# Float64 weights to float32: the sign by a slope of 2^32 and the low bits as integers on ScalarE

## The chip, the core and the metric

The kernel runs on one core of a Trainium2 chip. The metric is the device time of one execution in microseconds (us). A core has TensorE (PE in the profile, with its weight loads as PEld), VectorE (DVE), ScalarE (ACT), GpSimd (POOL) and SyncE (SP), which issues most of the transfers.

## What is computed

Attention with a sigmoid instead of a softmax feeds two dense layers, both of 768 to 2048 to 768 numbers for 1792 tokens:

```python
def _attn_ref(q, k, v):                     # 4 x 12 heads, 448 tokens, 64 numbers
    scores = scale * np.matmul(q, k.transpose(0, 1, 3, 2)) - np.log(S)
    return np.matmul(1.0 / (1.0 + np.exp(-scores)), v).astype(np.float32)

def _moe_ref(x, w_in, w_out):
    h = x @ w_in
    return ((h / (1.0 + np.exp(-h))) @ w_out).astype(np.float32)

def _moe2_ref(x, w_in, w_out, a, b):
    h = x @ w_in
    P = a[0] + a[1] * h + a[2] * h * h + a[3] * h * h * h
    Q = 1.0 + np.abs(b[0]) * np.abs(h) + np.abs(b[1]) * h * h
    return ((P / (Q + 1e-06)) @ w_out).astype(np.float32)
```

The four weight matrices arrive as float64, and the device reads them as pairs of 32-bit words, low word first. So the kernel itself turns 64 blocks of 128 x 768 numbers into float32: 16 blocks each of w_in and w_out of both layers.

## The kernel before

The stages follow each other on PE. Attention runs over 24 pairs of heads. The first product of layer one runs over 16 groups `g`, seven products `p1` to `p7` per group (a Strassen-like scheme, each product with nine matmuls of 448 columns, `product`, L552). The second product of layer one runs over 64 steps `n` of 18 matmuls (`second`, L699 to L701; blocks of 512, 384, 384 and 512 columns). Layer two follows with its first product (L772 to L774), the rational function, and its second product (L974). The order is written out by hand, and every engine works through its instructions in that order.

Each matmul operand is used as a high part and a rest: ACT casts a tile to the matmul type, and DVE (or POOL) subtracts that from the tile (`split`, L404 and L405; `split2`, L408 and L409; in the first product `split_later`, L414, and `flush`, L419). PE multiplies high by high, high by rest and rest by high.

A conversion of one block is issued by `conv` (L195 on). `conv_load` (L155 on) has SP load a block into a staging tile `t` of 128 x 768 x 2 words; `lo` and `hi` are its strided halves. `conv` then works in a tile `u` out of a ring of two (`bits`): ACT takes the absolute value of the high word, read as float32 (L204). DVE clamps it (L205), shifts it left by three bits and masks it (L206), puts the sign bit in (L209), and puts in the top three bits of the low word (L212). The last two read `hi` or `lo` with a stride of 8 bytes. `conv_out` (L177 on) then has SP store `u` to DRAM and load the next block; for seven blocks of w_out of layer one `conv_split` (L186 on) splits `u` at once into matmul operands instead. Both are put off to the next `conv_outs`.

With `parted=True` the last two DVE instructions are put off to `conv_rest`. The attention stage uses that form, for 12 blocks. The other 52 blocks are converted without it: 13 in the loop over `g`, one per group, and 39 in the loop over `n`, through `conv_to`, whose pace `conv_by` sets. ACT also issues the loads of `gd` and of the weights that are split in the loop over `n`.

Of the kernel before, what the change touches and what calls it, by code (L numbers as in the profile page):

```python
# [11 lines left out]
F32 = mybir.dt.float32  # L12
F32R = mybir.dt.float32r
I32 = mybir.dt.int32
AF = mybir.ActivationFunctionType
ALU = mybir.AluOpType
PSUM = bass.MemoryType.PSUM
# [5 lines left out]
MOST = (2.0 - 2.0**-3 - 2.0**-23) * 2.0**16  # L23
SIGN_TOP = -(1 << 30)
REST = 0x3FFFFFF8


class Ring:
# [13 lines left out]
def attention_moe_moe(ctx: ExitStack, tc: tile.TileContext, q, k, v, w_in1, w_out1, w_in2, w_out2, a, b2, out):  # L42
    nc = tc.nc
# [3 lines left out]
    P = 128  # L47
# [16 lines left out]
    cpool = ctx.enter_context(tc.tile_pool(name="cpool", bufs=1))  # L64
# [5 lines left out]
    def opened(name, side=None, space=None):  # L70
# [18 lines left out]
    xio = Ring([x_all[:, i, :] for i in range(3)])  # L89
    stage = Ring([t.bitcast(I32).rearrange("p (e t) -> p e t", t=2) for t in sb_[2 : 2 + NST]])  # L90
    bits = Ring(sb_[2 + NST : 4 + NST])
    xs = [[dr_p.tile([P, NT], F32, tag=f"xs{m}_{d}", name=f"xs{m}_{d}") for d in range(KD)] for m in range(2)]
    gd = [dr_p.tile([P, NT], F32, tag=f"gd{c}", name=f"gd{c}") for c in range(KF)]
    wd = [
        [{kind: dr_p.tile([P, DM], F32, tag=f"w{m}{kind}{c}", name=f"w{m}{kind}{c}") for kind in "io"} for c in range(KF)]
        for m in range(2)
    ]
# [18 lines left out]

    ident = cpool.tile([P, P], F32, tag="ident", name="ident")
    nls = cpool.tile([P, 1], F32, tag="nls", name="nls")
    ab = cpool.tile([P, 8], F32, tag="ab", name="ab")
    absb = cpool.tile([P, 2], F32, tag="absb", name="absb")  # L120
    nab = cpool.tile([P, 4], F32, tag="nab", name="nab")
# [3 lines left out]

    def constants():
        nc.vector.memset(nls, NEG_LOG_S)
        nc.vector.memset(lnb[:, 0:1], ONE * 2.0**-63)
        nc.vector.memset(lnb[:, 1:2], -63.0 * math.log(2.0))
        nc.scalar.activation(absb[:, 0:1], nls, AF.Sigmoid)  # L130
        make_identity(nc, ident)
# [6 lines left out]
    def coefficients_abs():  # L138
        nc.scalar.activation(absb, ab[:, 4:6], AF.Abs)
        nc.vector.tensor_scalar(nab, ab[:, 0:4], -1.0, 0.0, op0=ALU.mult, op1=ALU.add)  # L140

    WI = [w.bitcast(I32).rearrange("(k p) (f t) -> p k f t", p=P, t=2) for w in (w_in1, w_in2)]
    WO = [w.bitcast(I32).rearrange("(c p) (e t) -> c p e t", p=P, t=2) for w in (w_out1, w_out2)]
    order = [(0, "i", c + h * HF) for c in range(HF) for h in range(2)]
# [3 lines left out]
    staged = {}  # L150
    more = x_all.rearrange("p a b -> p (a b)").bitcast(I32).rearrange("p (e t) -> p e t", t=2)
    third = [None]
    done = {"load": 0, "conv": 0}
# [16 lines left out]
    outs = []  # L170
# [13 lines left out]
    direct = [KF]  # L184
# [8 lines left out]
    halves = []  # L193

    def conv(parted=False):  # L195
        i = done["conv"]
        if i >= len(order):
            return
        m, kind, c = order[i]
        t = staged.pop(i)  # L200
        lo, hi = t[:, :, 0], t[:, :, 1]
        u = bits.get()
        ui = u.bitcast(I32)
        nc.scalar.activation(u, hi.bitcast(F32), AF.Abs)  # L204
        nc.vector.tensor_scalar(u, u, LEAST, MOST, op0=ALU.max, op1=ALU.min)  # L205
        nc.vector.tensor_scalar(ui, ui, 3, REST, op0=ALU.logical_shift_left, op1=ALU.bitwise_and)  # L206

        def rest():
            nc.vector.scalar_tensor_tensor(  # L209
                out=ui, in0=hi, scalar=SIGN_TOP, in1=ui, op0=ALU.bitwise_and, op1=ALU.bitwise_or  # L210
            )
            nc.vector.scalar_tensor_tensor(  # L212
                out=ui, in0=lo, scalar=29, in1=ui, op0=ALU.logical_shift_right, op1=ALU.bitwise_or
            )
            outs.append(
                partial(conv_split, c, u, t)
                if (m, kind) == (0, "o") and c >= direct[0]
                else partial(conv_out, wd[m][c][kind], u, t)
            )

        done["conv"] += 1
        if parted:
            halves.append(rest)
        else:
            rest()

    def conv_rest():
        for do in halves:
# [3 lines left out]
    def conv_to(count):  # L232
        conv_outs()
        while done["conv"] < min(count, len(order)):
            conv_outs()
            conv()
# [133 lines left out]
    def attn_S(i, c, p):  # L370
        t = f2.get()
        nc.scalar.activation(t, p[:, :, :S], AF.Sigmoid, bias=nls, scale=QKSCALE)  # L372
        pairs.put(p)
# [196 lines left out]
    def silu(t, src, g, hi_f, second):  # L570
        nc.scalar.activation(t, src, AF.Silu)
        b = 2 * (g // HF) + second
        nc.sync.dma_start(out=gd[g % HF + hi_f * HF][:, b * S : (b + 1) * S], in_=t)
        f448.put(t)
# [213 lines left out]
    def act_a(n):  # L788
# [7 lines left out]
        for o, a1, _ in whole:  # L796
            nc.scalar.activation(a1, o, AF.Abs)
        nc.scalar.activation(q_, a_, AF.Identity, bias=B0, scale=B1)  # L798
# [220 lines left out]
    with tc.manual_schedule():  # L1019
# [14 lines left out]
        for i in range(4):  # L1034
            nc.vector.memset(ks_t[i][rest_of(i + 1), :, LAST * D :], 0.0)
        constants()
        warm(16)
        mix(0)
# [27 lines left out]
        for e, steps, units, new in quads():  # L1066
# [26 lines left out]
            for n in steps:  # L1093
# [30 lines left out]
                if n in CONVS:  # L1124
                    conv(True)
# [31 lines left out]
        for g in range(NGR):  # L1157
# [30 lines left out]
            if g and not HF - 1 <= g <= HF:  # L1188
                conv()
# [92 lines left out]
        for n in range(2, NL1):  # L1282
# [50 lines left out]
            m = n - (NL1 - KF)  # L1333
# [22 lines left out]
        def temps(w):  # L1356
            tm = [sb[:, i * 2 * w : (i + 1) * 2 * w] for i in range(sum(sizes) // (2 * w))]
            if w == BK:
                tm.insert(3, tm.pop(7))
            for ring, ts in ((us, tm[:4]), (aq, tm[4:8])):  # L1360
                ring.free.clear()
                ring.put(*ts)
            return tm[8:]

        rest = temps(BK)
# [6 lines left out]
        for n in range(HN):  # L1372
# [9 lines left out]
            if n == 2 * HF:  # L1382
                rest = temps(BK - P)
# [15 lines left out]
            if n == 3 * HF - 2:  # L1399
                gsrc.put(wif_all[:, NWS * HM : NWS * HM + BK])  # L1400
                load_g2(0)
                for i in range(2):
                    t = xa_all[:, 12 * BK + i * DM : 12 * BK + (i + 1) * DM]
# [88 lines left out]
```

## Time and profile before

| | us |
|---|---|
| median of 3 runs | 1035.62 |
| lowest and highest | 1034.79, 1036.03 |
| span of the profiled execution | 1036.1 |
| PE busy in it | 1026.3 |
| DVE busy in it | 783.3 |
| ACT busy in it | 606.1 |
| POOL busy in it | 273.5 |

The profile is one execution on the chip. Busy time is a sum over the span. A view by stages shows what an engine does in a stretch, the list of waits shows who stood idle until whom, and a timeline shows single instructions with their start. A matmul overlaps with the next one, so its duration in the profile is longer than the step from one start to the next; that step is its price.

### The profile page before, as it was taken

The page shows a single profiled execution, that of the slowest core. Times are in us where ns is not written, and L with a number is a line of the kernel's source. Part 1 is how long each engine was busy: PE and PEld are TensorE (multiplying, and loading weights), DVE is VectorE, ACT ScalarE, POOL GpSimd, SP SyncE. Part 2 cuts the span into 40 slices and gives each one's busy share as a digit, 9 for nine tenths or more (in the row PEclk, how much of TensorE's full clock was granted, in tenths as well). Part 3 has the DMA queues.
Part 4 walks back from the last instruction along what each step waited for, and adds up shares of the span by engine and source line. Part 5 has one row for each costly group of instructions (what it writes and reads, how often), then busy time and mean ns, then how long its engine had stood idle before and what let it go on. Part 6 is the DMA issues. An engine that isn't in the chain of part 4 may idle for free.

```text
span 1036.1 us, 16021 instructions
## 1 busy us (share of the span) xinstructions
PE 1026.3 (99%) x5568; PEld 894.5 (86%) x5568; DVE 783.3 (76%) x1101; ACT 606.1 (58%) x911; POOL 273.5 (26%) x242
## 2 busy tenths in 40 slices
PE   9999999999999999999999999999999999999998
PEld 6555547999999988899998888888999999999998
DVE  3788876888987759687867948879897968655761
ACT  5888876666655645233333458676778866454430
POOL 4335430000000000000000055778959922310000
PEclk9999999999999999999999999999999999999999
DMA  9989996777666856699989644566778878986641
GB/s 173 240 200 229 215 281 199 259 259 262 205 230 230 301 204 218 215 341 320 347 307 383 243 163 162 212 223 198 262 254 309 276 238 286 331 280 203 213 162 54
DMA packets 184081, 250.87 MB, mean 242 GB/s; under 512 B 57344, under 2 KB 136832, under 8 KB 184000
## 3 DMA queue, kind: packets, MB, share of 16 engines
q1 hardware_dynamic: 170080, 225.67, 67.5%
q10 hardware_dynamic: 11152, 17.36, 5.2%
q0 software_dynamic: 2768, 6.82, 2.9%
q8 instruction: 44, 0.72, 0.3%
q14 instruction: 37, 0.30, 0.1%
HBM read 166.17 MB, written 83.62 MB: 241 GB/s over the span
## 4 chain that ended last, share of the span: by engine, by line
PE 83%; DVE 8%; DMA 5%; ACT 2%; issue 1%; SPq 1%; POOL 0%; DVEq 0%; ACTq 0%; POOLq 0%
PE acc L552 14%; PE hp L974 14%; PE acc L701 6%; PE acc L699 6%; PE acc L700 6%; PE hb L552 5%; PE hb L974 5%; PE hp L774 5%; PE hp L772 5%; PE hp L773 5%; PE hb L381 4%; PE pair L357 3%; DMA sb<-in_moe_w_in_dram 3%; PE hb L701 2%; PE hb L700 2%; PE hb L699 2%
## 5 line engine op out<-in xcount | busy, mean ns | idle before, releaser
L204 ACT ACTIVATE sb<-sb 128x768 f32<-128x768 f32 x64 | 57.9, 905 | 72.7 <-DMA w1i<-sb 28.2
L699 PE MATMUL acc<-xa_all,woH 128*128 128x512 f32 (+1 forms) x252 | 91.9, 365 | 0.0
L700 PE MATMUL acc<-xa_all,woH 128*128 128x512 f32 (+1 forms) x252 | 91.9, 365 | 0.0
L701 PE MATMUL acc<-xa_all,woL 128*128 128x512 f32 (+1 forms) x252 | 91.9, 365 | 0.0
L372 ACT ACTIVATE sb<-pair,nls 128x896 f32<-128x896 f32 x84 | 80.1, 1006 | 7.9 <-PE pair L357 7.5
L409 POOL TENSOR_TENSOR woL<-wif,woH 128x768 fp32r<-128x768 f32 x9 | 16.5, 1848 | 248.1 <-DMA wif<-w1i 243.2
L801 POOL TENSOR_TENSOR sb<-sb 128x1024 f32<-128x1024 f32 (+1 forms) x32 | 69.6, 2174 | 39.0 <-ACT sb L798 39.0
L381 PE MATMUL hb<-sb,vs 128*64 128x448 f32 (+1 forms) x384 | 73.0, 554 | 0.0
L892 POOL TENSOR_TENSOR sb<-sb 128x384 f32<-128x384 f32 (+1 forms) x43 | 52.9, 1236 | 53.0 <-DMA sb<-gk 51.1
L552 PE MATMUL acc<-xb,wr 128*128 128x448 f32 x315 | 66.8, 362 | 0.0
L209 DVE SCALAR_TENSOR_TENSOR sb<-sb 128x768 int32<-128x768 int32 x64 | 65.3, 1021 | 1.8
L212 DVE SCALAR_TENSOR_TENSOR sb<-sb 128x768 int32<-128x768 int32 x64 | 63.3, 988 | 2.2
L552 PEld LDWEIGHTS acc<-xb,wr 128*128 128x128 f32 x315 | 59.0, 187 | 4.6 <-issue 0.7
L774 PE MATMUL hp<-hx,woL 128*128 128x512 f32 (+1 forms) x168 | 60.7, 362 | 0.0
L772 PE MATMUL hp<-hx,woH 128*128 128x512 f32 (+1 forms) x168 | 60.7, 362 | 0.0
L773 PE MATMUL hp<-hx,woH 128*128 128x512 f32 (+1 forms) x168 | 60.7, 362 | 0.0
L772 PE MATMUL hp<-xa_all,woH 128*128 128x512 f32 (+1 forms) x168 | 60.7, 362 | 0.0
L773 PE MATMUL hp<-xa_all,woH 128*128 128x512 f32 (+1 forms) x168 | 60.7, 362 | 0.0
L774 PE MATMUL hp<-xa_all,woL 128*128 128x512 f32 (+1 forms) x168 | 60.7, 362 | 0.0
L798 ACT ACTIVATE sb<-sb,absb 128x1024 f32<-128x1024 f32 (+1 forms) x32 | 36.4, 1139 | 33.5 <-DVE hb L819 33.2
L205 DVE TENSOR_SCALAR sb<-sb 128x768 f32<-128x768 f32 x64 | 36.5, 570 | 25.4 <-ACT sb L204 25.1
L803 DVE TENSOR_TENSOR sb<-hp,sb 128x768 f32<-128x768 f32 (+1 forms) x31 | 33.6, 1083 | 28.4 <-ACT sb L800 27.4
(246 smaller groups left out, 2769.9 us busy)
## 6 DMA issues: line engine op xcount, KB each, us to landing
sb<-in_moe_w_in_dram SPq DMA_DIRECT2D x32, 768.0 KB, 7.3
sb<-in_moe_w_out_dram SPq DMA_DIRECT2D x32, 768.0 KB, 6.8
gd<-sb SPq DMA_DIRECT2D x64, 224.0 KB, 3.5
wf<-w0i SPq DMA_DIRECT2D x32, 384.0 KB, 3.6
gk<-sb SPq DMA_DIRECT2D x28, 384.0 KB, 3.8
gk<-sb SPq DMA_DIRECT2D x15, 512.0 KB, 3.1
woL<-gk SPq DMA_DIRECT2D x25, 256.0 KB, 4.9
w0i<-sb SPq DMA_DIRECT2D x16, 384.0 KB, 4.0
```

Of the source, the lines that this page charges most:

```text
L209: nc.vector.scalar_tensor_tensor(out=ui, in0=hi, scalar=SIGN_TOP, in1=ui, op0=ALU.bitwise_and, op1=ALU.bitwise_or)
L372: nc.scalar.activation(t, p[:, :, :S], AF.Sigmoid, bias=nls, scale=QKSCALE)
L381: nc.tensor.matmul(hb[i_ % 2][j * D : (j + 1) * D, :S], vs[i_][part, j, c * D : (c + 1) * D], t[part, j], start=(c == 0), stop=(c == LAST),)
L552: nc.tensor.matmul(o, w_[:, w], x[:, i_, :], start=first and kk == 0 and n_ == 0, stop=kk == HK - 1 and n_ == 2, skip_group_check=not first,)
L699: nc.tensor.matmul(o, woH[c][:, w], x[:, 0, :w_], start=(c == 0), stop=False)
L700: nc.tensor.matmul(o, woH[c][:, w], x[:, 1, :w_], start=False, stop=False)
L701: nc.tensor.matmul(o, woL[c][:, w], x[:, 0, :w_], start=False, stop=(c == KF - 1))
L772: nc.tensor.matmul(o, wh[:, w], x[:, 0, :wd_], start=first, stop=False)
L773: nc.tensor.matmul(o, wh[:, w], x[:, 1, :wd_], start=False, stop=False)
L774: nc.tensor.matmul(o, wl[:, w], x[:, 0, :wd_], start=False, stop=last)
L801: nc.gpsimd.tensor_tensor(out=q_, in0=q_, in1=a_, op=ALU.mult)
L974: nc.tensor.matmul(o, a_, y[:, w_, :], start=kk_ == 0 and n_ == 0, stop=kk_ == HF - 1 and n_ == 2)
```

## The change

The conversion that is not parted gets another form. ACT's first pass scales the high word, read as float32, by 2^-112 and multiplies negative numbers by 2^32 on top (a Prelu with that slope). ACT's second pass reads the upper half of the low word as a 16-bit number x, and writes (x - 4095.5) / 8192, rounded to an integer, over the low word: its top three bits. DVE clamps the first result from both sides, and one combining instruction shifts it left by three bits and puts the three bits in. The shift drops the old sign bit; the factor 2^32 has put the sign into the exponent, from where the shift brings it to the top. A constant tile `mid` of one number per partition holds the bias of the second pass. The parted form stays as it was, and what follows a conversion (`kept_by`) is the same as before.

```diff
+DOWN = 2.0**-112
+NEGATIVE = 2.0**32
+MOST_DOWN = (2.0 - 2.0**-3 - 2.0**-23) * 2.0**-96
+EIGHTH = 2.0**-13
+MIDDLE = -4095.5 * 2.0**-13
...
+    mid = cpool.tile([P, 1], F32, tag="mid", name="mid")
...
         nc.vector.memset(nls, NEG_LOG_S)
+        nc.vector.memset(mid, MIDDLE)
...
+        kept_by = (
+            partial(conv_split, c, u, t) if (m, kind) == (0, "o") and c >= direct[0] else partial(conv_out, wd[m][c][kind], u, t)
+        )
+        done["conv"] += 1
+        if not parted:
+            nc.scalar.activation(u, hi.bitcast(F32), AF.Prelu, scale=DOWN, alpha=NEGATIVE)
+            nc.scalar.activation(lo, t.bitcast(U16)[:, :, 1], AF.Identity, bias=mid, scale=EIGHTH)
+            nc.vector.tensor_scalar(u, u, MOST_DOWN, -MOST_DOWN * NEGATIVE, op0=ALU.min, op1=ALU.max)
+            nc.vector.scalar_tensor_tensor(
+                out=ui, in0=ui, scalar=3, in1=lo, op0=ALU.logical_shift_left, op1=ALU.bitwise_or
+            )
+            outs.append(kept_by)
+            return
         nc.scalar.activation(u, hi.bitcast(F32), AF.Abs)
         nc.vector.tensor_scalar(u, u, LEAST, MOST, op0=ALU.max, op1=ALU.min)
         nc.vector.tensor_scalar(ui, ui, 3, REST, op0=ALU.logical_shift_left, op1=ALU.bitwise_and)
...
-            outs.append(
-                partial(conv_split, c, u, t)
-                if (m, kind) == (0, "o") and c >= direct[0]
-                else partial(conv_out, wd[m][c][kind], u, t)
-            )
-
-        done["conv"] += 1
-        if parted:
-            halves.append(rest)
-        else:
-            rest()
+            outs.append(kept_by)
+
+        halves.append(rest)
```

## Rows read from the trace of the kernel before

**Rows 1.** The page: busy time of the engines, and TensorE's granted clock in 40 slices.

```profile
PE 1026.3 (99%) x5568; PEld 894.5 (86%) x5568; DVE 783.3 (76%) x1101; ACT 606.1 (58%) x911; POOL 273.5 (26%) x242
...
PEclk9999999999999999999999999999999999999999
```

**Rows 2.** Busy time by stage: stretch, its length, each engine with its instructions.

```profile
163.00:373.00 210.00, 210.00 (x1048) 195.60 (x1045) 169.38 (x280) 126.59 (x229) 2.78 (x5) 1.00 0.71 238
373.00:595.00 222.00, 222.00 (x1116) 201.04 (x1115) 176.97 (x254) 90.00 (x138) 0.00 (x0) 1.00 0.84 294
```

**Rows 3.** The chain that ended last, in order of time: start, length, what.

```profile
193.89 12.60 PE acc L552 x63
```

**Rows 4.** Busy time of PE in two stretches; at the end clock, DMA share, GB/s.

```profile
377.25:426.21 48.96, 48.96 (x217) 1.00 0.67 227
433.44:477.12 43.68, 43.68 (x253) 1.00 0.98 334
```

**Rows 5.** Timeline of PE: start, length, line, tiles, form, count.

```profile
163.01 0.68 PE L552 MATMUL acc<-xb,wr 128*128 128x448 f32 x2
...
208.13 1.97 PE L552 MATMUL acc<-xa_all,wq 128*128 128x448 f32 x9
...
389.50 0.39 PE L699 MATMUL hb<-xa_all,woH 128*128 128x512 f32 x1
...
595.48 0.39 PE L772 MATMUL hb<-hx,w 128*128 128x512 f32 x1
```

**Rows 6.** Waits of PE and its weight loads, 163.1 to 595.4 us.

```profile
PEld acc L552 <- issue: 0.7, 1, 0.7
PEld hb L552 <- issue: 0.3, 1, 0.3
```

**Rows 7.** Conversions, 373 to 595 us, by line: count, busy us, mean ns, idle before.

```profile
L204 ACT ACTIVATE sb<-sb 128x768 f32<-128x768 f32 x39 | 35.4, 907 | 67.1 <-DMA w1i<-sb 28.2 <-DMA w1o<-sb 25.8 <-DVE xa_all L405 5.2
...
L212 DVE SCALAR_TENSOR_TENSOR sb<-sb 128x768 int32<-128x768 int32 x39 | 37.3, 957 | 1.4
L206 DVE TENSOR_SCALAR sb<-sb 128x768 int32<-128x768 int32 x39 | 21.9, 560 | 1.4
```

**Rows 8.** Other ACT groups by line and form.

```profile
L816 ACT ACTIVATE sb<-sb,lnb 128x768 f32<-128x768 f32 x16 | 14.8, 926 | 0.0
...
L408 ACT CAST woH<-sb 128x768 fp32r<-128x768 f32 x7 | 5.9, 836 | 15.8 <-DVE sb L212 15.8
...
L571 ACT ACT_TABLE_LOAD x1 | 1.3, 1283 | 0.0
```

**Rows 9.** Timeline of ACT in one group; in brackets the idle time before.

```profile
200.69 0.90 ACT L204 ACTIVATE sb<-sb 128x768 f32<-128x768 f32 x1
201.86 0.58 ACT L571 ACTIVATE sb<-sb 128x448 f32<-128x448 f32 x1 [0.27 <-DVE sb L426]
202.93 0.55 ACT L571 ACTIVATE sb<-acc 128x448 f32<-128x448 f32 x1 [0.49 <-PE acc L552]
203.37 0.51 ACT L414 CAST wq<-sf 128x384 fp32r<-128x384 f32 x1
204.73 0.53 ACT L627 COPY sb<-acc 128x448 f32<-128x448 f32 x1 [0.85 <-PE acc L552]
```

**Rows 10.** Timeline of DVE: the start of a conversion, and two low parts.

```profile
203.33 0.55 DVE L205 TENSOR_SCALAR sb<-sb 128x768 f32<-128x768 f32 x1
...
206.39 0.55 DVE L419 TENSOR_TENSOR wq<-sf,wq 128x384 fp32r<-128x384 f32 x1
...
388.38 0.68 DVE L405 TENSOR_TENSOR xa_all<-xa_all 128x512 fp32r<-128x512 f32 x1
```

**Rows 11.** Timeline of PE and DVE: matmuls while DVE is idle, DVE's next instruction.

```profile
368.65 0.39 PE L699 MATMUL acc<-xa_all,w 128*128 128x512 f32 x1
...
369.33 0.39 PE L699 MATMUL acc<-xa_all,w 128*128 128x512 f32 x1
...
373.38 0.62 DVE L426 TENSOR_TENSOR sb<-acc,sb 128x448 f32<-128x448 f32 x1 [7.53 <-PE acc L552]
```

More of the change, by code (lines that the diff above doesn't have):

```diff
@@ L14 @@
 I32 = mybir.dt.int32
+U16 = mybir.dt.uint16
 AF = mybir.ActivationFunctionType
```

## The prediction

> **What bounds the kernel now.** I read the page first, for the share of each engine and for TensorE's clock, and then left it, because a share over the whole span says nothing about one stage. PE is busy 99% and its granted clock is full in all 40 slices [rows 1]. Next came the table by stage [rows 2]. Of the 64 conversions, 12 run in the attention stage (0 to 163 us) in the parted form, which the change leaves alone. The other 52 lie in the two stages of the first MoE layer: 13 in its first products (163 to 373 us) and 39 in its second (373 to 595 us). Each iteration issues one or fewer of them. In both stages PE is busy the whole time, while DVE has 81% and 80% and ACT 60% and 41%.
>
> Busy PE need not be PE at its pace, so the next question is the distance from start to start. A run of 63 matmuls of 448 columns takes 12.60 us, 200.0 ns each [rows 3]. In the second stage 216 steps of 512 columns take 48.96 us, 226.7 ns each, and 252 steps of 384 columns take 43.68 us, 173.3 ns each (the counts in the rows hold one matmul more, which began before the stretch) [rows 4]. Laid end to end, 1008 x 0.2000 + 576 x 0.2267 + 576 x 0.1733 = 432.0 us. From the first matmul of the layer at 163.01 to the first of the next layer at 595.48 [rows 5] 432.5 us pass. So PE loses 0.5 us, and no more, in the whole stretch where the changed conversions run. The list of waits agrees: the only ones there are two of PE's weight loads, 0.7 and 0.3 us, put down to issue and to no engine [rows 6]. No row has PE waiting for a conversion.
>
> **The change, part by part.** All durations are from the profiled execution (span 1036.14 us; the runs have a median of 1035.62, so the trace is 0.05% above it and I take differences straight across).
>
> *Removed on DVE, for 52 conversions:* the shift with its mask (0.56 us) and one of the two combining instructions (0.96 us) [rows 7]. That is 1.52 us each, 79 us of DVE's 346 in the two stages. The clamp stays one instruction of the same form on the same tile (0.55 [rows 10]), the other combining instruction stays with the same operand layout (0.96).
>
> *Added on ACT, 52 times:* the first pass replaces the absolute value at 0.91 us; same data, same size, only the function differs. The second pass is new. No row shows a pass that reads every fourth 2-byte number and writes integers. The nearest is one of the same 768 numbers with a bias per partition, 0.93 us [rows 8], and I take that. From below, the plain cast of 768 numbers is 0.84 [rows 8]; I see no reason why it should cost nothing. From above, I allow twice the present strided pass, 1.81. So ACT gets 52 x 0.93 = 48 us (44 to 94) on top of 217.
>
> *On the path:* none of the 79 us saved is in front of PE, which loses 0.5 us in all. That is the ceiling of the gain. The cost is nil only as long as something hides it, so I checked the tightest places.
>
> First stage, one iteration. ACT does the absolute value at 200.69 and then the cast for the product p7 at 203.37; the copy of the sum at 204.73 waited 0.85 us for PE [rows 9]. DVE makes the low part of that cast at 206.39, right behind the conversion, and is done at 206.94 [rows 10]; p7 starts at 208.13 and reads the low part in its third matmul, 0.4 us later [rows 5]. The second ACT pass goes behind the first at about 201.5. Queued behind it on ACT are the two silu passes, the cast, the copy, the next weights' casts and the issues of loads; they move by at most 0.93, less the 0.27, 0.49 and 0.85 us that ACT stood waiting there [rows 9]. DVE's wait is new: its combining instruction now also needs the second ACT pass. But DVE reaches the conversion at 203.33 [rows 10], when that pass has been done for 0.9 us, and then is 1.5 us quicker. The low part moves from 206.94 to about 205.4 and the margin before p7 grows from 1.6 to about 3 us.
>
> Second stage. From the start of the ACT pass to the result a conversion took 0.91 + 0.55 + 0.56 + 0.96 + 0.96 and some gaps, 4.1 us. It becomes 0.91 + 0.93 on ACT and 0.96 behind it on DVE, 2.8 us. So SP, which issues the store of the result and then the next load, gets both 1.3 us sooner; it passes no other work, since the order on the queue is the same. ACT waits in this stage 54 us for those very stores to free a buffer [rows 7] and 16 us for DVE to finish a conversion before it casts the result [rows 8]; both waits shrink, by about as much as the pass costs. The tightest operand behind a conversion is the low part that DVE ended at 389.06 [rows 10] for a matmul at 389.50 [rows 5], 0.44 us. It came late because DVE was full; DVE is the engine that is relieved.
>
> *The rest:* the set of one constant in the first microsecond (DVE is idle until a load lands), and the small step by which the tiles allocated behind that constant move. Neither has a row; I take both as nothing.
>
> *Sum:* gain at most 0.5 us. If the new pass came whole in front of that 0.44 us twice, the loss is 2 x (0.93 - 0.44) = 1.0 us. I forecast no change, 1035.6 us.
>
> **The rivals.**
>
> *ACT becomes the bound of the second stage, slower.* The mechanism is the price of the added work per conversion there. ACT is busy 90.0 of 222 us [rows 2], so 39 conversions have room for (222 - 90) / 39 = 3.4 us each. Above that PE must wait. Against it: the row nearest to the pass is 0.93, and in the first stage even 4.7 us would still fit before p7. If the strided read and integer write were four times the present pass, 3.6 us, ACT would need 90 + 39 x 3.6 = 230 us and the time would be about 1044. The other way to that price is a reload of the function table around each new function: two loads of 1.283 us [rows 8] with the 0.93 make 3.5 us, 90 + 39 x 3.5 = 226 us, and about 1040. In its favour, the slope function appears nowhere in this trace; against it, absolute value, silu, sigmoid, casts and copies follow each other with three table loads in the whole run, of which the rows show one. The Trainium skill (ScalarE: Activation LUTs, section "Table sets: the hidden batching unit") says that tables are loaded as sets, that cheap functions such as relu, copy, identity and abs are in every set, and that a function outside the active set costs a load; it does not name the slope function among them. The trace agrees on the price, 1283 ns. Chance 0.05.
>
> *PE speeds up, faster.* The spacing of 200.0 ns is more than 448 columns take at the granted 2.4 GHz, 186.7 ns; the same 13.3 ns stand at 512 and 384. If DVE's traffic caused them, less of it would shorten 2160 matmuls by up to 13.3 ns, 29 us: 1007. Against it: DVE is idle for 7.53 us before 373.38, and there three matmuls of 512 columns still take 0.68 us, 227 ns each [rows 11], as when it works [rows 4]. The Trainium skill (Perfetto Trace Analysis, section "Identifying the Most-Contended Engine") says that busy time of matmuls is no good measure of the distance from the peak and that the busy share of weight loads is. By that rule there would be 14% left on PE (86% [rows 1]). The trace says that the rest is in the steady spacing, which this change does not touch. Chance 0.02.
>
> *The stores come earlier and collide with the loads of the operands.* From 433 us the DMA engines are 98% busy [rows 4]. An operand load that lands late would eat the margin of several microseconds that the casts have there, and then delay PE. The bytes are the same and the stores spread less densely only by 1.3 us each, so I expect at most 2 us: 1035.6 to 1038. Chance 0.03, two thirds of it above the bound.
>
> **How the numbers follow.** About 0.2%, 2.1 us, is what a measurement of this kernel can tell from no change. The forecast has 0.90 and stands at 1035.6. Its range goes from the lowest run less the ceiling of the gain, 1034.79 - 0.5 = 1034.3, to the highest run plus the loss, 1036.03 + 1.0 = 1037.0. It holds more than 8 in 10, so the rivals stay outside. Slower by more than the bound: 0.05 + 0.02 = 0.07. Faster: 0.02. The same: 0.91.
>
> **What the profile after would show.** Right, if PE is busy throughout from 163 to 595 us with the same spacing and the first matmul of the next layer starts 432 to 433 us after the first of this one; DVE loses about 79 us and ACT gains 44 to 94; ACT's waits for stores and DVE's results shrink; three table loads. The ACT rival would show as second passes of 3 us, or dozens of table loads, and PE waiting for casts in the second stage; the faster one as a spacing under 200 ns. A DVE clamp of a longer form would mean that the saving is smaller, with no effect on the time. The prediction is wrong if PE waits anywhere between 163 and 595 us for more than 2 us, or if the attention stage, which I take as untouched, changes its length.

## The result, and the profile after

The changed kernel takes 1042.88 us (median; 1039.68 to 1043.30) beside 1035.82 us for the kernel before (1034.79 to 1036.04): a ratio of 1.0070, with a 95% interval of 1.0049 to 1.0090. It is slower. The forecast was no change, with a range up to 1037.0. Measured again with more executions ("The change again" below), the ratio is 1.0038 (1.0021 to 1.0056). The two intervals overlap, and the second fits what the traces show.

The profiled execution of the changed kernel has a span of 1041.1 us. Lines of the code behind the conversion are 13 higher than before: L552 is L565, L699 is L712, L772 is L785, L974 is L987. The page shows that the load moved as intended:

```profile
PE 1029.5 (99%) x5568; PEld 894.8 (86%) x5568; DVE 699.2 (67%) x998; ACT 649.4 (62%) x963; POOL 271.5 (26%) x242
...
PEclk9999999999999999999999999999999999999999
```

DVE lost 84 us and ACT gained 43 [rows 1]. PE's granted clock is still full throughout. By stage, in the stretches of [rows 2] (stretch, length, busy time and instructions of PE, PEld, DVE, ACT, POOL, then PE's clock, DMA share, GB/s):

```profile
163.00:373.00 210.00, 209.62 (x1042) 194.72 (x1041) 150.50 (x254) 136.25 (x242) 2.79 (x5) 1.00 0.71 238
373.00:595.00 222.00, 222.00 (x1114) 200.87 (x1113) 120.09 (x175) 124.08 (x177) 0.00 (x0) 1.00 0.83 298
```

PE is busy nearly all the time in both, but it gets through 8 matmuls fewer (1042 + 1114 against 1048 + 1116). The groups of the new conversion, and the cast that follows some of them (count, busy us, mean ns, idle time before and its cause):

```profile
L218 ACT ACTIVATE sb<-sb,mid 128x768 int32<-128x768 uint16 x52 | 51.7, 993 | 0.0
L220 DVE SCALAR_TENSOR_TENSOR sb<-sb 128x768 int32<-128x768 int32 x52 | 49.9, 959 | 13.0 <-ACT sb L218 11.2 <-DMA sb<-in_moe_w_out_dram 0.3
L217 ACT ACTIVATE sb<-sb 128x768 f32<-128x768 f32 x52 | 46.6, 897 | 42.3 <-DMA w1i<-sb 24.0 <-issue 9.0 <-DMA w1o<-sb 8.2
...
L219 DVE TENSOR_SCALAR sb<-sb 128x768 f32<-128x768 f32 x52 | 29.0, 558 | 41.9 <-ACT sb L217 41.8
...
L421 ACT CAST woH<-sb 128x768 fp32r<-128x768 f32 x7 | 5.8, 834 | 1.2 <-DVE sb L220 1.2
```

Each is about as priced. ACT's waits for the stores fell from 54 to 32 us, and the cast's wait for DVE from 15.8 to 1.2 [rows 7, 8]. Nothing here explains a loss, and PE's waits (engine, tile, line, whom it waited for: total, times, longest), 163 to 592 us, hardly do:

```profile
PE hb L565 <- ACT sb L584: 0.4, 1, 0.4
PEld hb L565 <- ACT sb L584: 0.8, 1, 0.8
PEld hb L565 <- issue: 0.3, 1, 0.3
```

So the next reading is the start of each stage on PE's timeline (start, length, line, tiles, form, count). The kernel before, whose first two stage starts are in [rows 5], goes on with the first matmul of the last product and ends with the second line:

```profile
826.08 2.24 PE L974 MATMUL hp<-xa_all,hx 128*128 128x384 f32 x12
...
1031.76 0.79 PE L974 MATMUL hb<-w,hx 128*128 128x384 f32 x3
```

The changed kernel, the same four places:

```profile
162.56 0.68 PE L565 MATMUL acc<-xb,wr 128*128 128x448 f32 x2
...
596.38 0.39 PE L785 MATMUL hb<-hx,w 128*128 128x512 f32 x1
...
829.27 2.28 PE L987 MATMUL hp<-xa_all,hx 128*128 128x384 f32 x12
...
1036.77 0.79 PE L987 MATMUL hb<-w,hx 128*128 128x384 f32 x3
```

Attention became 0.45 us shorter. Layer one takes 433.82 us instead of 432.47 (+1.35), the first product of layer two 232.89 instead of 230.60 (+2.29), and the last product 208.29 instead of 206.47 (+1.82). From the end of attention to the end of the last matmul that is 875.0 against 869.5 us. Most of it is lost in layer two, which has no conversions at all.

What is slower there? Layer two's first product has 252 matmuls in a row that multiply `hx` by `woH` and `woL`, and later 252 that multiply `xa_all` by them. Busy time of PE in exactly these two stretches (stretch, length, busy time), before and after:

```profile
603.64:660.76 57.12, 57.12 (x253) 1.00 0.40 136
668.92:726.04 57.12, 57.12 (x253) 1.00 0.64 218
```

```profile
604.57:663.37 58.80, 58.80 (x254) 1.00 0.41 134
671.77:728.93 57.16, 57.16 (x254) 1.00 0.59 201
```

(The counts hold one or two that began before.) 57.12 / 252 is 226.7 ns a step, as in [rows 4]; `hx` by `woH` now takes 58.80 / 252 = 233.3 ns, `xa_all` by `woH` 226.8, as good as before. PE never stops in the slower stretch, waits for nobody and has its full clock; each of these matmuls is 6.6 ns longer. `woH`, `woL` and `xa_all` are allocated from the left end of SBUF (the on-chip memory), `hx` and `w` from the right. Nearly all of the loss falls on pairs across the two sides: the products of `xa_all` with `w` and the mixed ones of the last product too. Not every such pair pays: `hx` by `woH` with 384 columns keeps its 173 ns. Summed over all pairs of layers one and two, the longer steps make 4.1 us; some stalls make the other 1.4 of the 5.5.

The compiled kernels have the reason at hand. `mid` holds one number per partition, 4 bytes, and takes a slot of 32 bytes on the left side. Every left tile allocated after it moves by 32 bytes, and no right one does. In the compiled kernel before, `xa_all`, all of `woH` and `woL`, `hx` and `w` start 32 bytes past a multiple of 256. On the right a tile that nobody reads, `w0pad` (L1137, 448 bytes), sees to that: without it the right tiles would stand 192 bytes further, modulo 256. `mid` undid this order of the two sides.

### The profile page after: what moved, and what is told of

Same layout as the page of the kernel before. It is cut to its first block, busy times and chain, and to the rows that moved or that the text cites. A ratio compares the mean times of both kernels' runs of the same rounds, so it can differ in the third digit from the quotient of the medians.

```text
span 1041.1 us, 15974 instructions
## 1 busy us (share of the span) xinstructions
PE 1029.5 (99%) x5568; PEld 894.8 (86%) x5568; DVE 699.2 (67%) x998; ACT 649.4 (62%) x963; POOL 271.5 (26%) x242
## 4 chain that ended last, share of the span: by engine, by line
PE 73%; DVE 12%; DMA 7%; ACT 4%; issue 2%; SPq 1%; DVEq 0%; POOL 0%; ACTq 0%; POOLq 0%
PE acc L565 13%; PE hp L987 12%; PE acc L714 6%; PE acc L712 6%; PE acc L713 6%; PE hb L565 5%; PE hb L987 4%; PE hb L394 4%; PE pair L370 3%; PE hp L787 3%; PE hp L785 3%; PE hp L786 3%; DMA sb<-in_moe_w_in_dram 3%; DVE sb L818 2%; DVE sb L816 2%
## 5 line engine op out<-in xcount | busy, mean ns | idle before, releaser
L712 PE MATMUL acc<-xa_all,woH 128*128 128x512 f32 (+1 forms) x252 | 91.9, 365 | 0.0
L217 ACT ACTIVATE sb<-sb 128x768 f32<-128x768 f32 x52 | 46.6, 897 | 42.3 <-DMA w1i<-sb 24.0
L565 PE MATMUL acc<-xb,wr 128*128 128x448 f32 x315 | 66.9, 362 | 0.0
L565 PEld LDWEIGHTS acc<-xb,wr 128*128 128x128 f32 x315 | 59.0, 187 | 4.6 <-issue 0.7
L785 PE MATMUL hp<-hx,woH 128*128 128x512 f32 (+1 forms) x168 | 61.4, 366 | 0.0
L785 PE MATMUL hp<-xa_all,woH 128*128 128x512 f32 (+1 forms) x168 | 60.8, 362 | 0.0
L220 DVE SCALAR_TENSOR_TENSOR sb<-sb 128x768 int32<-128x768 int32 x52 | 49.9, 959 | 13.0 <-ACT sb L218 11.2
L219 DVE TENSOR_SCALAR sb<-sb 128x768 f32<-128x768 f32 x52 | 29.0, 558 | 41.9 <-ACT sb L217 41.8
L370 PEld LDWEIGHTS pair<-xa_all 64*128 64x128 f32 x384 | 33.8, 184 | 22.5 <-ACT sb L385 7.9
L714 PEld LDWEIGHTS acc<-xa_all,woL 128*128 128x128 f32 x252 | 47.3, 188 | 5.5
```

What stands on the lines that cost most here:

```text
L370: nc.tensor.matmul(p[:, j, :S], K[rows[j], a_, c * P : (c + 1) * P], Q[rows[j], b_, :], start=(n == 0), stop=(n == len(turns) - 1),)
L565: nc.tensor.matmul(o, w_[:, w], x[:, i_, :], start=first and kk == 0 and n_ == 0, stop=kk == HK - 1 and n_ == 2, skip_group_check=not first,)
L712: nc.tensor.matmul(o, woH[c][:, w], x[:, 0, :w_], start=(c == 0), stop=False)
L714: nc.tensor.matmul(o, woL[c][:, w], x[:, 0, :w_], start=False, stop=(c == KF - 1))
L785: nc.tensor.matmul(o, wh[:, w], x[:, 0, :wd_], start=first, stop=False)
```

## The experiments

Theory A: the loss is the address step. Theory B: the loss comes from the conversion's work, such as the passes on ACT. In the table, "distance" is by how much the distance between the left and the right tiles differs from that in the kernel before (left tiles move up and right tiles down, so it shrinks each time); "252 steps" are those of `hx` by `woH` and `woL`; "behind attention" is the time from the first matmul of layer one to the end of the last product.

| kernel | distance, bytes | 252 steps, us | behind attention, us | ratio to before (95%) |
|---|---|---|---|---|
| before | 0 | 57.12 | 869.5 | |
| the change | 32 | 58.80 | 875.0 | 1.0070 (1.0049 to 1.0090) |
| the tile alone | 32 | 58.80 | 874.2 | 1.0039 (1.0024 to 1.0054) |
| the conversion alone | 0 | 57.12 | 868.9 | 1.0006 (0.9988 to 1.0024) |
| kernel before, right side moved | 32 | 58.79 | 873.8 | 1.0031 (1.0016 to 1.0046) |
| the change, right side moved | 64 | 58.80 | 872.4 | 1.0027 (1.0013 to 1.0040) |
| the change, `mid` 256 bytes wide | 256 | 57.12 | 869.3 | 1.0006 (0.9991 to 1.0021) |
| the change again | 32 | 58.80 | 873.5 | 1.0038 (1.0021 to 1.0056) |

**The tile alone.** The kernel before with the tile added and set, and never read:

```diff
+    mid = cpool.tile([P, 1], F32, tag="mid", name="mid")
...
+        nc.vector.memset(mid, 0.0)
```

> Theory A (addresses): the kernel before with the constant tile alone, set but never read; the conversions keep their old four DVE instructions. The tile moves every tile allocated behind it on one side of the memory by one step of 32 bytes, against the tiles on the other side. If that is the cause, matmuls with one operand on each side take 233 ns at 512 columns (226.7 in the kernel before) and 175 to 177 at 384 (173.3), some 4 us in all by the spacing in the changed kernel's trace, and the time is 4 to 7 us above the kernel before. Theory B (the two ScalarE passes delay PE): no difference from the kernel before, spacing 226.7 and 173.3.

Measured: 1040.57 us, 1.0039. The 252 steps, in the view of PE's busy time:

```profile
603.67:662.47 58.80, 58.80 (x254) 1.00 0.45 151
```

The same pairs as in the changed kernel take the same longer steps, about 4 us in all. A tile that nobody reads brings the loss.

**The conversion alone.** The change, with its constant in a third column of a tile that was there, so that nothing moves:

```diff
-    mid = cpool.tile([P, 1], F32, tag="mid", name="mid")
-    lnb = cpool.tile([P, 2], F32, tag="lnb", name="lnb")
+    lnb = cpool.tile([P, 3], F32, tag="lnb", name="lnb")
+    mid = lnb[:, 2:3]
```

> The changed kernel with its constant in a spare column of a tile that is there already, so that no tile moves; the new conversions are complete. Theory A: spacing back to 226.7 and 173.3 ns, time within 1 us of the kernel before (0.5 us more for one wait for ScalarE in the first products, if that belongs to the conversions). Theory B: 5 to 7 us above the kernel before, as the changed kernel.

Measured: 1036.54 us, 1.0006. First the 252 steps, then the two products of layer one (all engines, as above):

```profile
599.98:657.10 57.12, 57.12 (x253) 1.00 0.37 120
...
159.12:357.71 198.59, 198.59 (x995) 185.68 (x991) 147.64 (x250) 132.70 (x236) 2.79 (x5) 1.00 0.73 244
357.71:591.82 234.11, 234.11 (x1171) 211.39 (x1170) 123.98 (x181) 128.02 (x184) 0.00 (x0) 1.00 0.81 291
```

All steps are those of the kernel before, and layer one takes 432.7 us (432.5 there). The new conversion itself costs nothing and brings nothing that 0.2% would show. Theory B falls.

**The other side moved.** Is it the address of the left tiles, or the distance between the two sides? The kernel before with 32 bytes put in at the right end:

```diff
+        spacer_p, _ = opened("spacer", side="right")
+        spacer_p.tile([P, 8], F32, tag="spacer", name="spacer")
```

> The kernel before with a spacer of 32 bytes on the other side, so that the tiles there move by 32 bytes and those on the first side stay. Theory A, if the distance between the two operands counts: spacing as in the changed kernel, 233 and 175 to 177 ns, 4 to 7 us slower. Theory A, if it is the absolute address of the first side's tiles that counts: as the kernel before. Theory B: as the kernel before.

```profile
599.96:658.75 58.79, 58.79 (x253) 1.00 0.45 150
```

Measured: 1038.69 us, 1.0031. By the medians that is 2.7 us and not the 4 to 7 expected; behind attention the trace has 4.2 us more. The left tiles stand where they stood in the kernel before, and the same pairs pay the same price. In the changed kernel `xa_all` by `woH`, where both tiles moved, kept its step. So the distance counts, not the address. The right side is filled downwards, so that this distance is 32 bytes as well.

**Both sides moved.** The change with the same two lines:

> The changed kernel, its tile kept, with the 32-byte spacer on the other side too: the two sides move apart by 64 bytes in all. Theory A, if the distance counts in steps of 64 bytes: spacing back to 226.7 and 173.3 ns and the time within 1 us of the kernel before. Theory A, if any move from the old distance costs, or the absolute address does: 4 to 7 us slower. Theory B: 5 to 7 us slower.

Measured: 1038.68 us, 1.0027. The 252 steps, and then 54 steps of 384 columns of the last product, which take 9.55 us in the changed kernel (965.05 to 974.60) and 9.36 in the one before (960.84 to 970.20):

```profile
604.78:663.58 58.80, 58.80 (x254) 1.00 0.41 135
...
964.48:973.85 9.37, 9.37 (x56) 1.00 0.69 219
```

The last product recovers, `hx` by `woH` does not: 64 bytes are another state, not the old one: `hx` by `woH` with 384 columns, which 32 bytes had spared, now takes 176.5 ns. None of the cases that I had written down came: the time is neither within 1 us of the kernel before nor 4 to 7 us above it, but 2.7 us. (The two sides also come closer by 64 bytes; they don't move apart.) That asked for a run over many distances.

**Many distances in one kernel.** The kernel before with 32 bytes behind every `woH` and `woL` tile, so that neighbouring weight blocks stand at different distances:

```diff
             woH.append(wo_p.tile([P, DM], F32R, tag=f"woH{c}", name=f"woH{c}"))
+            wo_p.tile([P, 8], F32, tag=f"gapH{c}", name=f"gapH{c}")
             woL.append(wo_p.tile([P, DM], F32R, tag=f"woL{c}", name=f"woL{c}"))
+            if c + 1 < KF:
+                wo_p.tile([P, 8], F32, tag=f"gapL{c}", name=f"gapL{c}")
```

> The kernel before with a gap of 32 bytes behind each of the 28 weight tiles of the second product, so that the distance between a weight tile and the operand that streams past it grows by 32 bytes from one weight block to the next, through all sixteen multiples of 32 within 512 bytes. Theory A: the step from matmul to matmul depends on that distance, 226.7 ns at 512 columns only where it is nothing modulo some power of two, and 229 to 235 at others (32 and 64 bytes gave 233); the pattern over the distances says modulo what. If the distance has no part in it, every block shows 226.7.

Measured, in one execution: 1046.5 us, beside 1034.4 for the kernel before on that chip. The 18 steps of each of the blocks 2 to 9, one line a block; `woH` is moved by 0, 64, 128 and so on bytes from line to line, `woL` by 32 more:

```profile
609.03:613.23 4.20, 4.20 (x20) 1.00 0.19 76
613.23:617.40 4.17, 4.17 (x20) 1.00 0.10 14
617.40:621.61 4.21, 4.21 (x20) 1.00 0.49 173
621.61:625.77 4.16, 4.16 (x19) 1.00 0.01 2
625.77:629.97 4.20, 4.20 (x20) 1.00 0.69 197
629.97:634.14 4.17, 4.17 (x20) 1.00 0.64 219
634.14:638.35 4.21, 4.21 (x20) 1.00 0.33 125
638.35:642.51 4.16, 4.16 (x19) 1.00 0.00 0
```

At 226.7 ns each line would be 18 x 0.2267 = 4.08. All are above it, and the lengths repeat after four lines, that is after 256 bytes. Averaged over the six like ones of a block, single steps of 512 columns went from 227 to 239 ns, and no block came out faster than in the kernel before, at 384 columns either.

The first and the fifth line hold something that theory A didn't expect. There `woH` has moved by 0 and by 256 bytes, so its twelve steps should make 2.72 us, and the six of `woL` would have to take 247 ns each to fill the 4.20. By the starts in the trace the two kinds of `woH` steps take 231 and 239 ns on average there, and that of `woL`, 32 bytes off, 230. So a matmul's own distance doesn't set its step alone; where the tiles of its neighbours lie counts too. Here `xa_all` by `woH`, both on the left, became slower as well (233.7 ns on average at 512 columns in layer one), so the sides as such don't matter.

**The whole change at a distance of 256 bytes.** If the period is 256, a wider tile must heal it, with nothing else undone:

```diff
-    mid = cpool.tile([P, 1], F32, tag="mid", name="mid")
+    mid_wide = cpool.tile([P, 64], F32, tag="mid", name="mid")
+    mid = mid_wide[:, 0:1]
```

> The whole change, but the tile mid is 256 bytes wide instead of 32, so that the left tiles move by 256 bytes against the right ones. Theory A (the step of a matmul depends on the distance between its weights and its moving operand, with a period of 256 bytes, as the repeat from block j to block j+4 in the kernel with spread tiles says): the steps come back to 226.7 ns at 512 columns and 173.3 at 384 in all six pairs, the sum of pace differences falls from +4.1 to under 0.3 us, attention end to end of the last product takes 869 to 870 us as in the kernel before, ratio 0.998 to 1.002. If the period is longer than 256 bytes (512, say): 228 to 239 ns in the pairs across the two sides, pace +3 to +6 us, ratio 1.003 to 1.007. If the passes on ScalarE were part of the cost (theory B): ratio 1.002 to 1.004 in spite of the steps of before.

```profile
600.92:658.04 57.12, 57.12 (x254) 1.00 0.37 120
957.50:966.86 9.36, 9.36 (x56) 1.00 0.71 216
```

Measured: 1036.67 us beside 1035.53, 1.0006, with all steps as before. The left tiles have moved, by 256 bytes, and it costs nothing. The tile and the setting of its constant are still there, so neither of these was the price.

**The change again**, on the same chip as the one above:

> The changed kernel once more, beside the one with the wide tile. Theory A: the moved tiles alone made 1.0039 (1.0024 to 1.0054) and the conversion alone 1.0006 (0.9988 to 1.0024), so 1.003 to 1.006 here; steps of 233.3 ns in the pairs across the two sides, pace +4.0 to +4.2 us against the kernel before, 873 to 875 us from the first matmul behind attention to the end of the last product. If the two parts add up to more than their sum: 1.007 or above, with PE waiting for over 2 us in the first layer.

```profile
602.39:661.19 58.80, 58.80 (x254) 1.00 0.41 136
```

Measured: 1039.55 us, 1.0038, 873.5 us behind attention, 4.0 more than before; the longer steps alone make 4.2. So the price of the moved tiles explains the loss here whole. The first measurement was 7.1 us, of which the trace showed 5.5 behind attention. What the rest was stays open. A candidate is the attention stage, whose code never changed: in eleven profiled executions, over all kernels, it ended between 158.6 and 164.3 us, in no order with the edits, and for the changed kernel itself once at 162.56 and once at 160.66. The 1.4 us of stalls in the first trace are not there in the second, so I count them as scatter too.

**How much room ACT has.** The prediction gave margins for the added pass. They are tested by doing the first pass several times over, on the kernel with the conversion alone; the repeated passes write the same numbers. Twice more, 2.8 us of new ACT work per conversion in all:

```diff
             nc.scalar.activation(u, hi.bitcast(F32), AF.Prelu, scale=DOWN, alpha=NEGATIVE)
+            nc.scalar.activation(u, hi.bitcast(F32), AF.Prelu, scale=DOWN, alpha=NEGATIVE)
+            nc.scalar.activation(u, hi.bitcast(F32), AF.Prelu, scale=DOWN, alpha=NEGATIVE)
```

> The new conversions with the constant in the spare column (no tile moves), and the first ScalarE pass made three times over (the same result each time): 2.8 us of ScalarE added per conversion instead of 1.0. My margin, 3.4 us per conversion in the second product of layer one, says: no change against the kernel before, within 0.2%. Theory B says slower by several microseconds.

Measured: 1041.10 us beside 1034.40, 1.0070 (1.0052 to 1.0088). The two products of layer one, and what PE and its weight loads waited for in the first of them:

```profile
160.79:363.08 202.29, 199.96 (x994) 185.27 (x991) 149.08 (x249) 153.53 (x262) 2.77 (x5) 1.00 0.71 240
363.08:597.24 234.16, 234.16 (x1171) 211.33 (x1170) 120.37 (x179) 193.22 (x259) 0.00 (x0) 1.00 0.82 285
```

```profile
PEld hb L567 <- ACT sb L586: 3.4, 5, 1.0
PEld hb L567 <- ACT sb L642: 1.2, 1, 1.2
...
PE hb L567 <- ACT sb L586: 1.2, 3, 0.6
PE hb L567 <- DVE sb L441: 0.8, 1, 0.8
```

The expectation of no change missed. The second product, with 39 conversions, takes the 234.2 us that it took without the extra passes (234.1). The first, with only 13, takes 3.7 us more. PE waits there for ACT's silu (L586) and copy (L642), which stand behind the conversion on ACT, and once for a sum on DVE (L441), not for the low part that I had followed. The name of a line tells who was late, not which operand or bank PE wanted; I didn't follow it further. The medians are 6.7 us apart; the profiled execution was the fastest of the four, 1038.47, and shows no more than these 3.7 us in layer one, so the rest stays open.

Four times more, 4.6 us per conversion:

> The same with the first ScalarE pass made five times: 4.6 us added per conversion, over the margin of 3.4 us in the second product of layer one. By the sum, ScalarE needs 90 + 39 x 4.6 = 269 us there against 222: PE waits and the time is some 40 to 50 us above the kernel before. If the margin is much larger than I worked out, no change.

```profile
158.82:381.52 222.70, 206.05 (x995) 188.55 (x991) 148.40 (x249) 176.80 (x290) 2.78 (x5) 0.98 0.65 217
381.52:652.77 271.25, 247.93 (x1171) 215.32 (x1171) 117.11 (x174) 253.08 (x328) 0.00 (x0) 0.97 0.74 245
```

Measured, in one execution: 1101.21 us, 67 more than the kernel before. The second product takes 271 us, as the sum of 269 said, with ACT busy 253 of them; that is 37 more than with the conversion alone. But the first costs 24 more as well, for which I had no term, so the 40 to 50 us missed. PE stands idle for 16.7 and 23.3 us in the two; the rest of the loss is busy time of PE, at a granted clock of 0.98 and 0.97.

## Why the prediction was wrong

*The step that failed* is in "The rest": "the small step by which the tiles allocated behind that constant move. Neither has a row; I take both as nothing." It was the only term that decided. Measured by itself it is 1.0039: 4.6 us by the medians, of which longer steps make about 4. The other unknown cost, the second pass on ACT, had a bound on both sides, and this one got none. With what the trace held, a bound could have been set: a step that changes by 1% in 5568 matmuls is worth 10 us. That the rows agreed at 226.7 and 173.3 ns said only that the present distances are equally good, not that any would be. And the code held a sign that I passed over: tiles that nobody reads, `qxpad` (L1030), `wrpad` (L1107) and `w0pad` (L1137), which do nothing but move others. It doesn't say what for.

*"The steady spacing, which this change does not touch"* fell with it. I treated the spacing as a constant of the engine, and looked in the rival of a faster PE only for traffic that might disturb it. The relief of DVE, the mechanism of that rival, did nothing. The place to see it is layer one, where the conversions ran: 252 steps of `xa_all` by `woH` and `woL` there, in the kernel before and with the conversion alone (stretch, length, busy time of PE, PEld, DVE, ACT, POOL):

```profile
373.18:430.30 57.12, 57.12 (x254) 47.31 (x253) 46.69 (x64) 27.27 (x42) 0.00 (x0) 1.00 0.62 210
369.52:426.64 57.12, 57.12 (x254) 47.32 (x253) 35.24 (x48) 34.47 (x50) 0.00 (x0) 1.00 0.62 210
```

DVE works 11 us less, and the steps stay at 226.7 ns.

*The ceiling of the gain held.* PE lost 0.5 us before, and the conversion alone is within the measurement of no change.

*DVE and ACT.* I took 79 us off DVE; the page has 84, of which 75 in layer one and most of the rest in layer two, which the change doesn't touch. I took 0.93 us for ACT's second pass (0.84 to 1.81); it is 0.993. At that price 52 passes are 51.7 us, but ACT's sum grew by 43 us, just under my 44 to 94. In the main this is because the second pass starts about 0.1 us before the first ends (378.40 + 0.91 against 379.21 for the first pair in the second stage), and busy time counts that once: some 5 of the 8 us. The Trainium skill (ScalarE: Activation LUTs, section "What ACT_TABLE_LOAD costs") gives 280 ns + 0.833 ns per element for a pass with a bias per partition, an estimate of 920 ns for 768, and about 93 ns of overlap between passes in a row. The bias pass of [rows 8] at 926 and the overlap agree; the strided 16-bit pass is 7% above that bias pass. Three table loads remained (L138, L584 and L1348), so the slope function needed none.

*The order of events around a conversion* went as worked out as far as the waits show it: ACT's waits for stores and for DVE shrank, and none of PE's waits in layer one names a DMA. DVE's new wait, which I had weighed for the first stage alone, is nothing there; in the second its combining instruction stands 11.2 us in all for the second ACT pass, and PE doesn't notice.

*The margins of the ACT rival* were half right. Above 3.4 us per conversion PE was to wait in the second stage: 2.8 cost nothing there and 4.6 cost 37 us. For the first stage I said that "even 4.7 us would still fit before p7", which followed one operand, the low part on DVE. The silu passes and the copy behind the conversion on ACT have less room, and 2.8 us already cost 3.7 us of time. With the real price, 0.99, it made no difference.

*The list of what would show it wrong* missed the case. PE didn't wait for more than 2 us between 163 and 595 us, and attention ended 0.45 us earlier, well inside its scatter. The one sign that spoke was "with the same spacing", and the first matmul of the next layer 433.8 us after the first of this one instead of 432 to 433; the larger part lay in layer two, to which no sentence of mine pointed.

## What to carry to other kernels

A new tile, however small, moves its neighbours; in a kernel bound by PE compare the step from matmul to matmul, pair of tiles by pair of tiles, before asking what the added work costs. Put a small constant into a spare column of a tile that is there, or pad the new tile until the distances are what they were (256 bytes here): both versions are as fast as the kernel before within 0.2%, and nothing tried was faster. A tile that nobody reads may be there for its length alone. Room on an engine is set by the first consumer behind the added work in its queue, so each one needs its own margin.

## What the runs showed of the hardware

The step of a matmul depends on where the tiles that PE reads lie in SBUF against each other. At 512 columns it is 226.7 ns in the kernel before and with the whole left side moved by 256 bytes. It is 233.3 ns for `hx` by `woH` with that side 32 or 64 bytes nearer, and from 227 to 239 ns where each weight tile stands at a distance of its own. With 384 columns it is 173.3 there, and from 171 to 180 between. The granted clock is full in all of them, and neither PE's waits nor its busy share show it.

The distance of a matmul's own two tiles is not the whole rule, as the run with many distances says: beside a `woL` tile 32 bytes off, an unmoved `woH` tile took 231 and 239 ns. Nor does every other distance cost. In the compiled kernel before, the weights of layer one's first product (`wr` and `wq`) stand 192 bytes past its other operands, modulo 256, and 448 columns take 200.0 ns [rows 3], with the same 13.3 ns over the prediction's 186.7 as the other widths. Which reads collide, a matmul's own operand with the load of the next weights or something else, no run here tells.

The Trainium skill (SBUF — State Buffer, section "SBUF: two separate sides") says that among the engines only the port pair of VectorE and GpSimd causes contention, and that PE never waits on anyone. For PE against DVE the conversion alone agrees: 75 us less of DVE's work in layer one, and the same 226.7 ns there. But PE's step is not free of where its own operands lie: 32 bytes made 233.3 ns of it.
